# A fused attention and mixture-of-experts kernel: two start-up softmaxes taken head by head on ScalarE, four loads in another order, and three kinds of low parts moved at the pair hand-overs

## The chip, the core and the metric

One core of one Trainium2 chip runs the whole kernel. The metric is device time in microseconds (us), the median of repeated runs. The core has five queues of instructions, each of which runs in order: TensorE (PE, with its weight loads as PEld), VectorE (DVE), ScalarE (ACT), GpSimd (POOL) and SyncE (SP), which here issues every DMA. They wait for one another by semaphores.

## What is computed

```python
# attention over chunks of 64 tokens, 8 heads of 64, batch 8, 576 tokens each
scores = scale * np.matmul(q_c, k_c.transpose(0, 1, 2, 4, 3))      # scale = 1/8
scores = scores - np.max(scores, axis=-1, keepdims=True)
attn = np.exp(scores)
attn = attn / (np.sum(attn, axis=-1, keepdims=True) + 1e-09)
out = np.matmul(attn, v_c)
# x: 4608 tokens x 512; 4 experts, each 512 -> 1024 -> 512, weighted densely
p = domain_probs / (domain_probs.sum(-1, keepdims=True) + 1e-09)
for e in range(E):
    h = np.maximum(x @ w1[e], 0.0)
    out += p[:, e:e + 1] * (h @ w2[e])
```

All is fp32 at the outside.

## The kernel before

The 4608 tokens are nine blocks of 512. The first block is handled alone; the other eight form four pairs of blocks. The experts are cut into eight passes (`n_pass`: expert and half of the hidden width), so that the program is 40 passes: 8 for the first block, then 8 for each pair. Every matrix product is made of three fp32r products of a high part and a low part: `hi_part` is a cast on ScalarE, `lo_part` is a subtraction (source minus high part) on VectorE or GpSimd. From the first pair on, products of 1024 x 1024 are made with seven instead of eight block products (sums of blocks named s1 to s4 for weights, t1 to t4 for tokens), so blocks b11, b21, b22, t1 to t4 of the tokens need high and low parts each.

**The order is written by hand.** Inside `tc.manual_schedule()` each engine runs its instructions in the order of the code. Three places matter here.

*The start* (`load_all`, `startup`). Block 0 is four tiles of 128 tokens (t = 0 to 3). `load_all` issues the loads on SyncE. `startup` keeps TensorE busy with idle products (`keep_warm`, 128x512 in bf16 into a bank that nobody reads) until the first data is there. For tile 0 and tile 1: `start_scores` (32 products of 64x64 into one PSUM bank, 8 heads of 64 columns), `less_max` on VectorE (a maximum per head, L185, then its subtraction from all 512 columns, L187), `a_exp` on ScalarE (one exp of 128x512, L190), and `start_weights`, which is `a_norm` on VectorE: sum per head (L193), plus 1e-9 (L194), reciprocal (L196), product (L198). Then come transpose (L841, copied out of PSUM on ScalarE at L845), `start_values` (L854, attention times v), `start_x` (the high part of x, L278 on ScalarE) and `start_x_lo` (its low part, L281 on VectorE). `w1_split` makes the parts of a quarter of w1 (cast at L278, subtraction at L281). `start_hidden` makes the first products of w1 with x, for the tiles 0 and 1 together. Tiles 2 and 3 follow in the same way between these products.

*A pass* (`later_pass`). 28 steps, the list `WOVEN`, stand in TensorE's order: g and h are products of w1 (left) with token parts (right), a and b are products of w2 with the hidden parts of the pass ahead. Each is six matmuls of 128x512. Extra work is hung behind a step with `add(at, step, ...)`. After an a or b step `Outer.add` (L697) adds the PSUM bank to the accumulator on VectorE; the next product into the same bank waits for that.

*The hand-over from pair to pair.* In the last pass of a pair (`last_pass and more`, twice in the program: pair 1 to pair 2 after pass 23, and once more after pass 31; the first pair gets its parts elsewhere) the token parts of the next pair are made from `xraw` with the methods of `Tokens`: t2 lies in the two tiles `e` and `pt` (`sum2_apart`) and gets its parts in `split2` (L441) at step 20. The parts that are needed last are made in the list `late`, which is hung into the steps of the following pass: low part of t3 behind step 1, of t4 behind step 4, of b22 behind step 7. The first pass of the new pair reads t2 at step 4 (g6), t1 at step 6 (g5), t3 at step 9 (g7), t4 at step 11 (g4), b22 at step 12 (g3).

Of the kernel before, what the change touches and what calls it, by code (L numbers as in the profile page):

```python
# [15 lines left out]
P = 128  # L16
C = 64
# [4 lines left out]
NK = 4  # L22
HF = 512

WAITS = {"loads": 7, "softmax": 14, "copy": 2}
PAIR = 2
N_RAW = 6

# [2 lines left out]
def chunk_attention_moe(ctx: ExitStack, tc: tile.TileContext, qk, v, v0, dp, w1, w2, out):  # L31
# [241 lines left out]
    def w_loads(i, n, order=QUADS):  # L273
        for f, k in order:
            w_load(i, n, f, k)
# [7 lines left out]
    def split(eng, src, t):  # L283
        hi_part(src, t)
        lo_part(eng, src, t)
# [119 lines left out]
    class Tokens:  # L405
# [35 lines left out]
        def split2(self):  # L441
            i = self.KEYS["t2"]
            x_alloc(i)
            for k, t in enumerate(self.t2):
                split(nc.vector, t, [part[:, k] for part in xt[i]])

        def sum3(self, eng=None):
            self.less("t3", "b22", "b12", self.b12, eng)
# [365 lines left out]
    def start_load(t, step):  # L814
        for g in range(0, 2, step):
            b = slice(g, g + step)
            nc.sync.dma_start(
                out=qk0[t][:, b], in_=qk[t, b].rearrange("g c d x h s -> (c d) g x h s")
            )

    def start_v(t):
        nc.sync.dma_start(out=v0s[t // GT], in_=v0[:, t : t + GT])
# [76 lines left out]
    def load_all():  # L899
        start_load(0, 1)  # L900
        start_load(1, 2)
        start_v(0)
        start_load(2, 2)
        w_loads(0, 0)
        start_load(3, 2)
        start_v(2)
        nc.sync.dma_start(out=pr, in_=dp)
        w_load(1, 0, 0, 0)
        w_load(1, 0, 0, 1)

    def start_weights(t):
        es[t] = att.tile([P, 2 * HG, C], F32, name=("e", "pt")[t % 2])
# [2 lines left out]
    def startup(beside):  # L915
# [4 lines left out]
        keep_warm(WAITS["loads"], early)  # L920
        for t in range(2):
            start_scores(t)
            less_max(sc[t])
            a_exp(sc[t])
        start_weights(0)
        start_weights(1)
        keep_warm(WAITS["softmax"])
        start_transpose(0)
        for f, k in QUADS[:2]:
            w1_split(f, k, nc.gpsimd)  # L930
        keep_warm(WAITS["copy"])
        start_values(0)
        start_x(0)
        start_transpose(1)
        w1_split(1, 0, nc.gpsimd)
        start_x_lo(0)
        start_scores(2)
        less_max(sc[2])
        start_values(1)
        start_x(1)  # L940
        a_exp(sc[2])
        w1_split(1, 1, nc.gpsimd)
        start_x_lo(1)
# [283 lines left out]
    def later_pass(n, ahead, late, held):  # L1227
# [42 lines left out]
        if last_pass and more:  # L1270
# [11 lines left out]
            add(at, 26, lambda: x.hi("t4"))  # L1282
            late = [
                (0, lambda: x.hi("b22")), (0, lambda: first_load(pair + 2)), (1, lambda: x.lo("t3")),
                (4, lambda: x.lo("t4")), (7, lambda: x.lo("b22")),
            ]
        for i, name in enumerate(WOVEN):
            getattr(steps[name[0]], f"p{name[1]}")()
# [133 lines left out]
```

## Time and profile before

| what | before |
|---|---|
| median of three runs | 1523.82 us (1523.77 to 1523.97) |
| profiled execution | 1523.9 us, its span 1522.1 us (1.8 us lie around the span) |
| busy share of PE / DVE / ACT / POOL | 99% / 61% / 38% / 58% |
| chain that ended last | PE 94%, DVE 4%, DMA 1% |
| granted TensorE clock | 0.999 on the mean |

The profile is one execution on the chip. "Busy" is time in which an engine worked on an instruction; an idle time is put down to the instruction that ended it. The chain that ended last is followed back from the last instruction. Start times are counted from the start of the span.

### The profile page before, as it was taken

Reading aid. Unit: us, or ns where it says so; the run is one execution under the profiler, and the core shown is the slowest. Engines: PE = TensorE matmul, PEld = TensorE weight load, DVE = VectorE, ACT = ScalarE, POOL = GpSimd, SP = SyncE. Lnnn points to the kernel's source line nnn. Section 1 sums busy time; section 2 is a strip of 40 time slices with the busy share of each in tenths; the row PEclk is TensorE's granted clock in tenths of the full one; section 3 lists DMA queues with packets and bytes.
Section 4 is the critical chain, followed back from the end, with each engine's and each line's share of the span. In section 5 each row is a group of like instructions: output and inputs, shape, how many; then the busy total and the mean of one; then the engine's idle time right before and its main releaser. Section 6 shows DMA issues by size and latency. Waiting matters only on the chain.

```text
span 1522.1 us, 23390 instructions
## 1 busy us (share of the span) xinstructions
PE 1508.0 (99%) x8863; PEld 1239.0 (81%) x8863; DVE 922.0 (61%) x1290; ACT 573.1 (38%) x1000; POOL 875.7 (58%) x666
## 2 busy tenths in 40 slices
PE   8999999999999999999999999999999999999998
PEld 7888888888888888888888788888887788888887
DVE  5453554444444465776677956666668756666665
ACT  3343444344444434333333444333333443333332
POOL 2443578677666626555557654555557655555554
PEclk9999999999999999999999999999999999999999
DMA  6353349777677576766666667666666676666664
GB/s 196 125 158 123 111 163 312 267 254 243 227 238 237 195 262 214 230 208 220 216 195 197 194 231 236 209 227 213 207 192 199 191 231 201 198 202 200 201 193 140
DMA packets 167920, 314.17 MB, mean 206 GB/s; under 512 B 14192, under 2 KB 84096, under 8 KB 167808
## 3 DMA queue, kind: packets, MB, share of 16 engines
q1 hardware_dynamic: 167808, 312.68, 63.6%
q8 instruction: 70, 1.15, 0.3%
q14 instruction: 42, 0.34, 0.1%
HBM read 244.39 MB, written 68.23 MB: 205 GB/s over the span
## 4 chain that ended last, share of the span: by engine, by line
PE 94%; DVE 4%; DMA 1%; issue 0%; ACT 0%; POOL 0%; SPq 0%; DVEq 0%; ACTq 0%
PE A L468 46%; PE C L468 27%; PE B L468 16%; PE psa L169 1%; DVE xl L281 1%; PE psa L140 1%; PE psa L160 1%; DVE acc L697 1%; DVE wraw L641 1%; DMA wraw<-in_w 1%; PE psa L783 0%; DVE wraw L635 0%; DVE B L670 0%; DVE xraw L438 0%; PE A L854 0%
## 5 line engine op out<-in xcount | busy, mean ns | idle before, releaser
L650 POOL TENSOR_TENSOR hfl<-wraw,hfh 128x512 fp32r<-128x512 f32 x288 | 377.1, 1325 | 221.2 <-ACT hfh L647 218.9
L468 PE MATMUL A<-xh,wf 128*128 128x512 f32 (+1 forms) x1112 | 380.7, 389 | 0.3 <-DVE acc L763 0.3
L468 PE MATMUL A<-hfh,wf 128*128 128x512 f32 (+1 forms) x768 | 271.0, 394 | 2.7 <-DVE acc L697 2.7
L647 ACT CAST hfh<-wraw 128x512 fp32r<-128x512 f32 x288 | 176.5, 622 | 214.7 <-DVE wraw L641 64.0
L468 PEld LDWEIGHTS A<-xh,wf 128*128 128x128 f32 x1112 | 207.9, 188 | 43.2 <-issue 0.4
L530 ACT COPY s<-A 128x512 f32<-128x512 f32 x192 | 112.8, 587 | 329.9 <-PE A L468 329.2
L468 PE MATMUL A<-xl,wf 128*128 128x512 f32 (+1 forms) x556 | 214.8, 387 | 0.0
L468 PE MATMUL C<-xh,wf 128*128 128x512 f32 (+1 forms) x592 | 202.9, 390 | 0.0
L468 PEld LDWEIGHTS A<-hfh,wf 128*128 128x128 f32 x768 | 144.2, 188 | 34.2 <-DVE acc L697 4.6
L697 DVE TENSOR_TENSOR acc<-A,acc 128x512 f32<-128x512 f32 x174 | 119.3, 686 | 78.7 <-PE A L468 78.2
L468 PE MATMUL A<-hfl,wf 128*128 128x512 f32 x384 | 149.5, 389 | 0.0
L468 PE MATMUL C<-hfh,wf 128*128 128x512 f32 x384 | 134.4, 391 | 2.1 <-DVE acc L697 2.1
L281 POOL TENSOR_TENSOR hfl<-wraw,hfh 128x512 fp32r<-128x512 f32 x64 | 86.0, 1373 | 82.9 <-ACT hfh L278 80.9
L468 PEld LDWEIGHTS C<-xh,wf 128*128 128x128 f32 x592 | 110.5, 188 | 22.9
L468 PE MATMUL B<-xh,wf 128*128 128x512 f32 (+1 forms) x376 | 124.6, 385 | 0.7 <-ACT xh L278 0.7
L281 POOL TENSOR_TENSOR wf<-wraw,wf 128x512 fp32r<-128x512 f32 x70 | 91.3, 1327 | 52.7 <-ACT wf L278 52.4
L468 PEld LDWEIGHTS A<-xl,wf 128*128 128x128 f32 x556 | 104.3, 188 | 21.2
L468 PE MATMUL C<-xl,wf 128*128 128x512 f32 (+1 forms) x296 | 114.1, 387 | 0.0
L641 POOL TENSOR_TENSOR wf<-wraw,wf 128x512 f32<-128x512 f32 x23 | 29.7, 1293 | 143.9 <-DVE wf L635 143.9
L697 DVE TENSOR_TENSOR acc<-C,acc 128x512 f32<-128x512 f32 x90 | 62.0, 690 | 63.0 <-PE C L468 57.5
L650 POOL TENSOR_TENSOR hfl<-wf,hfh 128x512 fp32r<-128x512 f32 x48 | 70.9, 1478 | 37.7 <-ACT hfh L647 37.4
L468 PEld LDWEIGHTS C<-hfh,wf 128*128 128x128 f32 x384 | 72.1, 188 | 17.9 <-DVE acc L697 3.0
(194 smaller groups left out, 2733.2 us busy)
## 6 DMA issues: line engine op xcount, KB each, us to landing
wf<-w SPq DMA_DIRECT2D x336, 512.0 KB, 4.0
wraw<-in_w SPq DMA_DIRECT2D x128, 256.0 KB, 4.0
w<-wf SPq DMA_DIRECT2D x112, 256.0 KB, 4.3
qk_in<-in_qk SPq DMA_DIRECT2D x32, 512.0 KB, 5.6
v_in<-in_v SPq DMA_DIRECT2D x32, 256.0 KB, 4.3
w<-hfl SPq DMA_DIRECT2D x32, 256.0 KB, 2.4
w<-hfh SPq DMA_DIRECT2D x32, 256.0 KB, 2.9
w<-hfh SPq DMA_DIRECT2D x48, 128.0 KB, 2.6
```

The lines of the kernel that those rows point to most:

```text
L140: nc.tensor.matmul(s["sc"][half, c, j], lhsT=s["x"][rows, g, 0, h], rhs=s["x"][rows, g, 1, h], start=True, stop=True,)
L160: nc.tensor.transpose(ps[:, j], s["e"][:, j].rearrange("p c k -> p (c k)"), ident)
L169: nc.tensor.matmul(av[half, c, j], lhsT=s["v"][rows, 2 * j + odd], rhs=s["pt"][rows, j, half], start=True, stop=True,)
L281: eng.tensor_tensor(out=t[1], in0=src, in1=t[0].bitcast(F32), op=ALU.subtract)
L468: nc.tensor.matmul(out, lhsT=lhs(k, a), rhs=rhs(k, b), start=first and i == 0, stop=last and i == len(parts) - 1, skip_group_check=not (fi ...
L530: nc.scalar.copy(out=t, in_=self.a)
L641: (eng or nc.vector).tensor_tensor(out=self.values[place, k], in0=self.values[a, k], in1=self.values[b, k], op=op)
L647: nc.scalar.copy(out=self.part(name, 0)[:, k], in_=self.values[name, k])
L650: (eng or nc.gpsimd).tensor_tensor(out=self.part(name, 1)[:, k], in0=self.values[name, k], in1=self.part(name, 0)[:, k].bitcast(F32), op=A ...
L697: nc.vector.tensor_tensor(out=acc[key], in0=src, in1=acc[key], op=ALU.add)
```

## The change

**At the start.** The exps of tiles 0 and 1 go to a new `start_exp`: VectorE takes the maximum of each head and multiplies it by -1/8 (128x8), and ScalarE takes exp(x/8 + that) head by head, eight instructions of 128x64, each with an accumulated sum of the head (`accum_out`). `start_norm` adds 1e-9, takes the reciprocal and multiplies. Subtraction and sum over 128x512 on VectorE are gone for these two tiles. The idle products ahead of the first transpose are 10 instead of 14. The loads of w1's first two quarters stand ahead of that of tile 2. The parts of these two quarters are made behind the copies of both tiles, the second's low part on VectorE instead of GpSimd, and the scores of tile 2 stand behind the values of tile 1.

**At the hand-overs.** `split2` makes t2's two low parts on GpSimd; the low parts of t4 and b22 stand behind steps 6 and 8 instead of 4 and 7.

```diff
-WAITS = {"loads": 7, "softmax": 14, "copy": 2}
+WAITS = {"loads": 7, "softmax": 10, "copy": 2}
...
-                split(nc.vector, t, [part[:, k] for part in xt[i]])
+                split(nc.gpsimd, t, [part[:, k] for part in xt[i]])
...
+        w_load(0, 0, 0, 0)
+        w_load(0, 0, 0, 1)
         start_load(2, 2)
-        w_loads(0, 0)
+        w_load(0, 0, 1, 0)
+        w_load(0, 0, 1, 1)
...
+    def start_exp(t):
+        a, scale = sc[t], 1.0 / C**0.5
+        m = small.tile([P, 2 * HG], F32, name="m3")
+        nc.vector.tensor_reduce(out=m, in_=a, op=ALU.max, axis=AX)
+        nc.vector.tensor_scalar_mul(m, m, -scale)
+        zs[t] = small.tile([P, 2 * HG], F32, name="z3")
+        for h in range(2 * HG):
+            nc.scalar.activation(
+                out=a[:, h], in_=a[:, h], func=AF.Exp, scale=scale,
+                bias=m[:, h : h + 1], accum_out=zs[t][:, h : h + 1],
+            )
+
+    def start_norm(t):
+        es[t] = att.tile([P, 2 * HG, C], F32, name=("e", "pt")[t % 2])
+        z = zs[t]
+        nc.vector.tensor_scalar_add(z, z, 1e-9)
+        nc.vector.reciprocal(out=z, in_=z)
+        nc.vector.tensor_tensor(
+            out=es[t], in0=sc[t], in1=z.unsqueeze(2).broadcast_to(sc[t].shape), op=ALU.mult
+        )
...
             start_scores(t)
-            less_max(sc[t])
-            a_exp(sc[t])
-        start_weights(0)
-        start_weights(1)
+            start_exp(t)
+        start_norm(0)
+        start_norm(1)
         keep_warm(WAITS["softmax"])
         start_transpose(0)
-        for f, k in QUADS[:2]:
-            w1_split(f, k, nc.gpsimd)
         keep_warm(WAITS["copy"])
         start_values(0)
         start_x(0)
         start_transpose(1)
-        w1_split(1, 0, nc.gpsimd)
+        w1_split(0, 0, nc.gpsimd)
+        w1_split(0, 1, nc.vector)
         start_x_lo(0)
-        start_scores(2)
-        less_max(sc[2])
         start_values(1)
         start_x(1)
+        start_scores(2)
+        w1_split(1, 0, nc.gpsimd)
+        less_max(sc[2])
         a_exp(sc[2])
...
-                (4, lambda: x.lo("t4")), (7, lambda: x.lo("b22")),
+                (6, lambda: x.lo("t4")), (8, lambda: x.lo("b22")),
```

What stands in a row on the engines now, at the three places that the prediction speaks of:

ScalarE at the start, before (A are the scores of tiles 0 and 1, B and the first A banks behind them their transposes and values, C the scores of tile 2, `s` the copied transposes, `wf` the high parts of w1, `xh` those of x; in brackets the semaphores waited for):

```order
L190 ACTIVATE A_249<-A_249 128x512 [waits DVE_49,PE_49]
L190 ACTIVATE A_270<-A_270 128x512 [waits DVE_49,PE_49]
L845 COPY s_322<-B_317 128x512 [waits PE_49]
L278 CAST wf_324<-wraw 128x2x256 [waits DMAHW5_49]
L278 CAST wf_327<-wraw 128x2x256 [waits DMAHW6_49]
L278 CAST xh_238<-B_332 128x4x128 [waits PE_49]
L845 COPY s_355<-B_350 128x512 [waits PE_49]
L278 CAST wf_357<-wraw 128x2x256 [waits DMAHW7_49]
L278 CAST xh_238<-A_381 128x4x128 [waits PE_49]
L190 ACTIVATE C_361<-C_361 128x512 [waits DVE_49]
```

ScalarE at the start, after:

```order
L924 ACTIVATE A_249,z_269<-A_249,m_266 128x64 [waits DVE_49,PE_49]
L924 ACTIVATE A_249,z_269<-A_249,m_266 128x64 [waits Activation_49] x7
L924 ACTIVATE A_278,z_298<-A_278,m_295 128x64 [waits DVE_49,PE_49]
L924 ACTIVATE A_278,z_298<-A_278,m_295 128x64 [waits Activation_49] x7
L845 COPY s_330<-B_325 128x512 [waits PE_49]
L278 CAST xh_238<-B_334 128x4x128 [waits PE_49]
L845 COPY s_357<-B_352 128x512 [waits PE_49]
L278 CAST wf_359<-wraw 128x2x256 [waits DMAHW4_49]
L278 CAST wf_362<-wraw 128x2x256 [waits DMAHW5_49]
L278 CAST xh_238<-A_366 128x4x128 [waits PE_49]
```

Sixteen exps stand where two stood, and all but the first of a tile wait for ScalarE's own semaphore, that is for the exp ahead of them; the casts of w1 moved behind both copies.

GpSimd at a hand-over, before (`hfl` are low parts of the hidden values, L650):

```order
L650 TENSOR_TENSOR hfl_8273<-wraw,hfh_8271 128x512
L650 TENSOR_TENSOR hfl_8300<-wf_8176,hfh_8298 128x512
L650 TENSOR_TENSOR hfl_8318<-wraw,hfh_8316 128x512
L650 TENSOR_TENSOR hfl_8333<-wraw,hfh_8331 128x512
L650 TENSOR_TENSOR hfl_8273<-wraw,hfh_8271 128x512
L650 TENSOR_TENSOR hfl_8333<-wraw,hfh_8331 128x512
```

The same after:

```order
L650 TENSOR_TENSOR hfl_8281<-wraw,hfh_8279 128x512
L281 TENSOR_TENSOR xl_8284<-e,xh_8283 128x512
L281 TENSOR_TENSOR xl_8284<-pt,xh_8283 128x512
L650 TENSOR_TENSOR hfl_8308<-wf_8184,hfh_8306 128x512
L650 TENSOR_TENSOR hfl_8326<-wraw,hfh_8324 128x512
L650 TENSOR_TENSOR hfl_8341<-wraw,hfh_8339 128x512
L650 TENSOR_TENSOR hfl_8281<-wraw,hfh_8279 128x512
L650 TENSOR_TENSOR hfl_8341<-wraw,hfh_8339 128x512
```

The two low parts of t2 now stand ahead of the five low parts that close the pass; the last two of these with one name (8333 before, 8341 after) are read by step a2 of the next pass.

VectorE in the first pass after a hand-over, before (the first `xl` is t4's, the second b22's):

```order
L697 TENSOR_TENSOR acc_5735<-B_8403,acc_5735 128x512
L670 TENSOR_TENSOR B_8413<-B_8413,s_8398 128x512
L635 SCALAR_TENSOR_TENSOR wraw<-B_8413,ws 128x512
L281 TENSOR_TENSOR xl_8362<-xraw,xh_8361 128x1024
L697 TENSOR_TENSOR acc_5820<-C_8439,acc_5820 128x512
L697 TENSOR_TENSOR acc_5843<-A_8377,acc_5843 128x512
L281 TENSOR_TENSOR xl_8387<-xraw,xh_8386 128x1024
L697 TENSOR_TENSOR acc_5843<-C_8439,acc_5843 128x512
```

The same after:

```order
L697 TENSOR_TENSOR acc_5743<-B_8411,acc_5743 128x512
L670 TENSOR_TENSOR B_8421<-B_8421,s_8406 128x512
L635 SCALAR_TENSOR_TENSOR wraw<-B_8421,ws 128x512
L697 TENSOR_TENSOR acc_5828<-C_8446,acc_5828 128x512
L281 TENSOR_TENSOR xl_8370<-xraw,xh_8369 128x1024
L697 TENSOR_TENSOR acc_5851<-A_8385,acc_5851 128x512
L697 TENSOR_TENSOR acc_5851<-C_8446,acc_5851 128x512
L281 TENSOR_TENSOR xl_8395<-xraw,xh_8394 128x1024
```

Each of the two low parts moved behind one addition of a C bank.

## Rows read from the trace of the kernel before

**Rows 1.** The page, busy time, share and count by engine.

```profile
PE 1508.0 (99%) x8863; PEld 1239.0 (81%) x8863; DVE 922.0 (61%) x1290; ACT 573.1 (38%) x1000; POOL 875.7 (58%) x666
```

**Rows 2.** What TensorE waited for in the span: us in total, times, longest.

```profile
PE A L468 <- DVE acc L697: 2.7, 2, 1.3
PE C L468 <- DVE acc L697: 2.1, 2, 1.1
```

**Rows 3.** Timeline of ScalarE, start: start us, us, what, [idle before <-releaser].

```profile
11.37 0.58 ACT L845 COPY s<-B 128x512 f32<-128x512 f32 x1 [1.91 <-PE B L841]
13.03 0.62 ACT L278 CAST wf<-wraw 128x512 fp32r<-128x512 f32 x1 [1.07 <-DMA wraw<-in_w]
```

**Rows 4.** Timeline of VectorE, start.

```profile
5.59 0.69 DVE L185 TENSOR_REDUCE m<-A 128x8 f32<-128x512 f32 x1 [4.18 <-PE A L830]
...
9.41 0.17 DVE L194 TENSOR_SCALAR psa<-psa 128x8 f32<-128x8 f32 x1
...
15.63 0.68 DVE L185 TENSOR_REDUCE m<-C 128x8 f32<-128x512 f32 x1
...
19.13 0.69 DVE L198 TENSOR_TENSOR e<-C,z 128x512 f32<-128x512 f32 x1
20.66 0.69 DVE L185 TENSOR_REDUCE m<-C 128x8 f32<-128x512 f32 x1 [0.84 <-PE C L830]
```

**Rows 5.** Timeline of TensorE, start.

```profile
12.01 1.15 PE L854 MATMUL B<-s,qk_in 64*64 64x64 f32 x32 [0.24 <-ACT s L845]
...
13.09 0.66 PE L841 MATMUL B<-ident,pt 128*128 128x128 f32 x4
13.67 1.15 PE L830 MATMUL C<-xraw 64*64 64x64 f32 x32
...
23.86 1.15 PE L854 MATMUL A<-s,ws 64*64 64x64 f32 x32 [0.23 <-ACT s L845]
```

**Rows 6.** Groups of ScalarE by shape: busy us, mean ns of one | idle.

```profile
L190 ACT ACTIVATE A<-A 128x512 f32<-128x512 f32 x2 | 1.2, 582 | 6.1 <-DVE A L187 6.1
...
L103 ACT COPY s<-B 128x128 f32<-128x128 f32 x1 | 0.3, 266 | 2.9 <-PE B L102 2.9
...
L919 ACT ACTIVATE first<-s 128x1 f32<-128x1 bf16 x1 | 0.2, 203 | 0.0
```

**Rows 7.** Timeline of VectorE at the first hand-over.

```profile
850.21 1.18 DVE L281 TENSOR_TENSOR xl<-e,xh 128x512 fp32r<-128x512 f32 x1
...
851.91 0.68 DVE L697 TENSOR_TENSOR acc<-A,acc 128x512 f32<-128x512 f32 x1
...
855.04 1.27 DVE L281 TENSOR_TENSOR xl<-qk_in,xh 128x1024 fp32r<-128x1024 f32 x1
...
866.91 1.63 DVE L281 TENSOR_TENSOR xl<-xraw,xh 128x1024 fp32r<-128x1024 f32 x1
868.47 0.68 DVE L697 TENSOR_TENSOR acc<-C,acc 128x512 f32<-128x512 f32 x1
```

**Rows 8.** Timeline of GpSimd at the first hand-over.

```profile
828.81 2.54 POOL L650 TENSOR_TENSOR hfl<-wraw,hfh 128x512 fp32r<-128x512 f32 x2
...
841.07 3.52 POOL L650 TENSOR_TENSOR hfl<-wraw,hfh 128x512 fp32r<-128x512 f32 x2 [3.27 <-ACT hfh L647]
...
853.92 1.30 POOL L650 TENSOR_TENSOR hfl<-wraw,hfh 128x512 fp32r<-128x512 f32 x1 [3.08 <-ACT hfh L647]
855.39 4.59 POOL L650 TENSOR_TENSOR hfl<-wraw,hfh 128x512 fp32r<-128x512 f32 x3 [0.17 <-ACT hfh L647]
```

**Rows 9.** Timeline of TensorE at the first hand-over: two stops, and steps a2 and g2.

```profile
852.65 0.50 PE L468 MATMUL A<-hfh,wf 128*128 128x512 f32 x1 [1.33 <-DVE acc L697]
...
859.84 0.39 PE L468 MATMUL B<-hfh,wf 128*128 128x512 f32 x1
...
861.19 0.39 PE L468 MATMUL B<-xh,wf 128*128 128x512 f32 x1
...
869.21 0.50 PE L468 MATMUL C<-hfh,wf 128*128 128x512 f32 x1 [1.05 <-DVE acc L697]
```

More of the change, by code (lines that the diff above doesn't have):

```diff
@@ L909, in load_all @@
         w_load(1, 0, 0, 1)
+    zs = {}
+    def start_exp(t):
[17 more added lines that the diff above has]
+        )
     def start_weights(t):
```

## The prediction

> **What bounds the kernel now.** I read the page's busy times first: TensorE is busy for 1508.0 of the 1522.1 us of the span, VectorE for 922.0, ScalarE for 573.1, GpSimd for 875.7 [rows 1]. So nothing but TensorE's idle time can be won, 14.1 us in all. Second, what TensorE waited for: the two largest items are two kinds of stop before an addition of VectorE, 2.7 us in 2 times and 2.1 us in 2 times [rows 2], one of each kind at either hand-over between pairs. The rest of the idle time lies in the start and at the end. The change touches the start and the hand-overs, so I read both from the timelines. At the start TensorE is not lost to its own work but to a chain that goes round all engines (scores, maximum, exp, norm, transpose, copy, values), and it ends with the values of tile 2 at 23.86 us [rows 5]; behind that TensorE runs without a gap worth naming, so what this point moves, the end moves.
>
> **The start.** The old chain has for each tile a maximum, a subtraction and one exp of 0.58 us [rows 6]. The new one has a maximum (0.69) and a product of 128x8, which I take at the 0.17 of the like instruction [rows 4]; with hand-offs of some 0.05 the first exp begins at 5.59 + 0.69 + 0.17 + 0.07 = 6.52 us, where the old one began 0.6 us later. Then come sixteen exps on ScalarE, one behind the other, since each waits for the one ahead (the order, second list). Call the time from one to the next c. No row shows an exp with a bias from memory and a sum beside it. ScalarE's rows fall with the columns, 0.582 for 512 and 0.266 for 128 [rows 6]; the same slope gives 0.21 for 64, with a hand-off of 0.04 c = 0.25, the low end. If giving out the sum takes an instruction of its own, as long as the shortest on ScalarE, 0.203 [rows 6], and its hand-off, c = 0.49, the high end. I see no reason for either end and take the middle, 0.37.
>
> The Trainium skill has a rule that speaks against the change (ScalarE: Activation LUTs, section Rules for kernel authors): some 0.3 us for every ACTIVATE with a bias as a [128,1] pointer, plus 0.83 ns an element, which for 64 columns would be an estimated 0.35, and c an estimated 0.39. The rows of this kernel, whose bias is no pointer, lie lower (0.582 for 512 columns, where the rule would say 0.72), so no run here shows it yet; the sum would come out 0.3 us higher by it.
>
> ScalarE runs in order, so the first copy of a transpose stands behind both tiles' exps: S = 6.57 + 16c, which is 12.5 us at c = 0.37 against 11.37 [rows 3]. From S on: values of tile 0 begin 0.64 later (as 11.37 to 12.01) and take 1.15, transpose of tile 1 0.66 [rows 5], its copy until S + 3.1, values of tile 1 until S + 4.3, scores of tile 2, now behind them, until S + 5.4. VectorE meanwhile: ScalarE casts w1's first quarter at S + 2.95, GpSimd begins the low part at S + 3.6 and needs 1.27, half of 2.54 [rows 8]. VectorE's low part of the second quarter is due at S + 4.1, but the two engines take turns on such instructions (a GpSimd pair takes 3.52 instead of 2.54 beside VectorE's [rows 8]), so it runs to S + 5.5, the low part of x's first tile to S + 6.1, and the maximum of tile 2 starts there. Before, that maximum started at 15.63, the norm of tile 2 ended at 19.82, then VectorE waited 0.84 for the scores of tile 3, and from that maximum at 20.66 to the values at 23.86 it is 3.20 [rows 4, 5]. In the new order the scores of tile 3 are done earlier (S + 8.6) than the norm of tile 2 (S + 10.3), so the wait is gone: 4.19 + 3.20 = 7.39. The values of tile 2 begin at S + 13.5 = 20.07 + 16c, against 23.86: **a loss of 16c - 3.8**, which is 0.2 at the low end, 2.1 at 0.37, 4.0 at the high end. The chain won 0.6 on VectorE and lost it on ScalarE, and moving tile 2's scores behind tile 1's values lengthened it.
>
> What else the start changes costs nothing while this holds. w1's first half loaded earlier: before, ScalarE waited for it until 13.03 [rows 3] with both copies queued behind; now the cast is not due before S + 2.95 = 15.4, so the load is early in either order, and at c = 0.25 (13.5) still not late. Tile 2's load is 0.5 MB later; its scores ran at 13.67 without a wait [rows 5] and are due at S + 4.3 = 16.8. On SyncE the w2 loads that reuse w1's buffers are issued some 2 us later, and their casts are later as well. Four idle products fewer only shorten filling. The norms (0.17, then about 0.9) end before TensorE asks for them.
>
> **The hand-overs.** The first stop, 1.33 at 852.65 [rows 9], ended with the addition of 851.91, which stands 1.70 us behind the start of t2's low parts at 850.21 [rows 7]. Without them it ends 1.70 earlier and the stop is gone. But the two go to GpSimd at 1.27 each. GpSimd was idle for 3.08 us there, until 853.92, and then did four low parts, the last until 859.98 [rows 8]. That fits, but VectorE gets its turns in between. From 849.6 (853.92 - 3.08 - 1.27) GpSimd now has seven of 1.27, 8.9 us, and in it two of VectorE's 512-column sums at some 0.6 and t1's low part at some 1.2 (rows of 0.68 and 1.27 with their overlap [rows 7]): it ends at about 860.9, 0.9 later than before. Step a2 reads that last low part in the fifth of its six matmuls; they lie (861.19 - 859.84) / 6 = 0.23 apart, so at 859.84 + 4 x 0.23 = 860.75 [rows 9]. So TensorE wins 1.33 at the first stop and gives it back at a2: 0 is my value. The bounds are 1.4 won, if GpSimd gets through ahead of VectorE, and 0.2 lost.
>
> The second stop, 1.05 at 869.21, waits for the C addition of 868.47; t4's low part stands right ahead of it and held it from 866.91, 1.56 [rows 7, 9]. Moved behind, the addition may be 1.56 - 1.05 = 0.5 later for other reasons before TensorE stops again. GpSimd's later turns delay t3's low part by about 0.5, so the stop all but vanishes: 1.0 won. Who waits next: t4's low part now delays the addition that the next A product waits for, and b22's (up to 2.4 us with a turn of GpSimd's) ends close to step g3, which reads it. For that 0 to 0.8 may be lost. A hand-over thus wins 1.0, bounds 0.2 to 2.4 (both stops whole), and there are two: **2.0 won, 0.4 to 4.8**.
>
> **The sum.** The profiled execution took 1523.9 us; its median sister runs 0.1 less. 1523.9 + 2.1 - 2.0 - 0.1 = **1523.9 us**: no difference that can be told, since a measurement of this kernel tells about 0.2%, 3.05 us, from no change.
>
> **The rivals.** (1) *Cheap exps*: c is 0.25 to 0.30, ScalarE overlaps what the rows suggest it doesn't. For: the fall of the rows to 0.266 at 128 columns. Against: sixteen waits in a row. The start loses 0.6, the hand-overs win 2.0: 1522.4. (2) *The hand-overs clear wholly*: GpSimd takes t2's parts in its idle 3.08 us, no stop comes back, 4.8 won. For: the gap is longer than two parts. Against: the turns, and a2's nearness. With c = 0.37 1521.1, with cheap exps 1519.6. (3) *The accumulated sums are dear*, the case that ends slower: every exp is followed by a second instruction and c is 0.49 or more. Its place is ScalarE between 6.5 us and the first copy; it is slower than before as soon as 16c - 3.8 exceeds the hand-overs' 2.0, c > 0.36, and by more than 0.2% from c = 0.55. At 0.49 the time is 1525.8, at 0.57 1527.1; with hand-overs that win only 0.4, 0.49 gives 1527.4. (4) *The stops only move*: b22's or GpSimd's parts come late and the hand-overs win 0.4 in all; 1525.5.
>
> **How the numbers follow.** Forecast (c from 0.31 to 0.45, 1 us won at a hand-over) 0.42; (1) 0.18; (2) 0.12; (3) 0.18; (4) 0.10. Faster by over 0.2% (below 1520.8) takes nearly all of (2) when the exps are not dear, and little else: 0.11. Slower by over 0.2% (above 1526.9) takes most of (3) and a part of (4): 0.15. The same 0.74. The range goes from 1520.9 (two clear hand-overs, middling exps) to 1527.0 (exps near 0.56).
>
> **What would show it.** Right: exps of tile 0 and 1 that begin near 6.5 and follow each other by 0.31 to 0.45; the first copy of a transpose near 12.5; the maximum of tile 2 near 18.6 and the values of tile 2 near 26 us. At 850 to 853 no stop of TensorE, but one of about 1 us in step a2 that GpSimd's low part ends; the stop at the third addition below 0.3. Wrong: a c outside 0.31 to 0.45, a cast of w1 that waits for its DMA, no stop in a2, or one before t4's or b22's product.

## The result, and the profile after

The changed kernel takes 1526.28 us (median of 22 executions, 1524.18 to 1527.45) against 1523.86 (22 of the kernel before): ratio 1.0013, 95% interval 1.0007 to 1.0019. That lies inside the 0.2% that the prediction called "no difference that can be told", and inside its range; the forecast of 1523.9 is 2.4 us too low. The interval lies wholly above 1, so the change is a small loss and not nothing. The executions do not scatter round the median. Nine lie at 1524.18 to 1524.62 (mean granted clock 0.999), two at 1525.8 and eleven at 1526.8 to 1527.5 (all thirteen at 0.996 or 0.997), and the median falls into the gap. The profiled execution (1527.19 us, span 1525.5) is one of the upper ones.

What TensorE waited for (us in total, times, longest), which answers [rows 2]:

```profile
PE B L841 <- DVE e L934: 2.1, 1, 2.1
PE B L468 <- POOL hfl L650: 1.6, 2, 0.8
...
PE C L468 <- DVE B L670: 0.7, 2, 0.3
PE A L468 <- DVE acc L697: 0.5, 2, 0.2
```

The two old items, 2.7 and 2.1 before an addition, have shrunk to 0.5 and nothing. GpSimd's 1.6 is new at the hand-overs, with 0.7 behind it. Two large waits are new in the start: 2.1 us before the first transpose and 1.5 before the first values (the latter in TensorE's timeline below).

**Hand-overs.** TensorE and GpSimd at the first one, timelines (start us, us, what, idle before and what ended it), against [rows 8, 9]:

```profile
860.97 0.50 PE L468 MATMUL A<-hfh,wf 128*128 128x512 f32 x1 [0.23 <-DVE acc L697]
865.71 0.50 PE L468 MATMUL B<-hfl,wf 128*128 128x512 f32 x1 [0.82 <-POOL hfl L650]
879.04 0.50 PE L468 MATMUL C<-xh,wf 128*128 128x512 f32 x1 [0.33 <-DVE B L670]
```

```profile
854.44 1.75 POOL L281 TENSOR_TENSOR xl<-e,xh 128x512 fp32r<-128x512 f32 x1
856.14 1.83 POOL L281 TENSOR_TENSOR xl<-pt,xh 128x512 fp32r<-128x512 f32 x1
```

0.23 + 0.82 + 0.33 = 1.38 stand where 1.33 + 1.05 = 2.38 stood [rows 9]: 1.0 won at a hand-over, 2.0 at the two, the forecast to the tenth. GpSimd's two new parts take 1.75 and 1.83 instead of 1.27; into each falls an instruction of VectorE with two inputs from SBUF (L438 until 855.02, L641 from 856.14 to 856.81).

**Start.** ScalarE's timeline, then the groups of its new instructions (busy us, mean ns of one):

```profile
7.30 0.29 ACT L924 ACTIVATE A<-A,m 128x64 f32<-128x64 f32 x1 [5.07 <-DVE m L921]
7.51 0.19 ACT L924 ACTIVATION_READ_ACCUMULATOR A<-A,m 128x1 f32 x1
7.74 0.29 ACT L924 ACTIVATE A<-A,m 128x64 f32<-128x64 f32 x1
...
10.36 0.29 ACT L924 ACTIVATE A<-A,m 128x64 f32<-128x64 f32 x1
...
10.67 0.28 ACT L924 ACTIVATE A<-A,m 128x64 f32<-128x64 f32 x1
...
14.03 0.57 ACT L845 COPY s<-B 128x512 f32<-128x512 f32 x1
```

```profile
L924 ACT ACTIVATE A<-A,m 128x64 f32<-128x64 f32 x16 | 4.6, 287 | 5.5 <-DVE m L921 5.1
L924 ACT ACTIVATION_READ_ACCUMULATOR A<-A,m 128x1 f32 x16 | 3.1, 193 | 0.0
```

Each exp is followed by a second instruction that gives out its sum, as the high end of the prediction assumed. From one exp to the next it is 0.44 us, except at one place: the first exp of tile 1, which waits for no exp ahead of it, starts 10.67 - 10.36 = 0.31 behind the last of tile 0. The sixteen fill 14.03 - 7.30 = 6.73 us, so c = 0.42 on the mean. The first copy of a transpose starts at 14.03 (forecast 12.5, before 11.37 [rows 3]).

TensorE in the same stretch, against [rows 5]:

```profile
4.28 1.97 PE L830 MATMUL A<-xraw 64*64 64x64 f32 x32
...
12.08 0.63 PE L841 MATMUL B<-ident,e 128*128 128x128 f32 x4 [2.14 <-DVE e L934]
...
14.66 1.97 PE L854 MATMUL B<-s,qk_in 64*64 64x64 f32 x32 [1.52 <-ACT s L845]
16.56 1.11 PE L841 MATMUL B<-ident,pt 128*128 128x128 f32 x4
...
29.22 1.15 PE L854 MATMUL A<-s,ws 64*64 64x64 f32 x32 [0.23 <-ACT s L845]
```

The ten idle products end at 12.08 - 2.14 = 9.94, and TensorE then stands still until 12.08. Behind that the same kinds of product take nearly twice as long as before: values of 32 instructions 1.97 instead of 1.15, a transpose 1.11 instead of 0.66. The values of tile 2 start at 29.22 instead of 23.86. The reason is in the view by stretches (stretch, us, TensorE's busy time, granted clock, DMA share and GB/s):

```profile
12.00:14.00 2.00, 1.06 (x6) 0.87 1.08 397
14.00:16.00 2.00, 1.34 (x26) 0.50 1.06 381
16.00:18.00 2.00, 1.67 (x16) 0.50 0.47 155
...
20.00:22.00 2.00, 2.00 (x40) 0.50 0.31 99
22.00:24.00 2.00, 2.00 (x12) 0.57 0.72 203
24.00:26.00 2.00, 2.00 (x41) 1.00 0.90 326
```

The granted clock is 0.50 of full speed, the 1.2 of TensorE's two levels (1.2 and 2.4 GHz), from 14 to 22 us. In the kernel before every one of these stretches reads 1.00, as here:

```profile
12.00:14.00 2.00, 1.99 (x46) 1.00 0.94 283
```

The span's account closes: the start loses 29.22 - 23.86 = 5.36, the hand-overs win 2.0, and the span grew by 1525.5 - 1522.1 = 3.4.

### The profile page after: what moved, and what is told of

Read it like the earlier page. It is cut to its first block, busy times and chain, and to the rows that moved or that the text cites. A ratio compares the mean times of both kernels' runs of the same rounds, so it can differ in the third digit from the quotient of the medians.

```text
span 1525.5 us, 23412 instructions
## 1 busy us (share of the span) xinstructions
PE 1511.6 (99%) x8859; PEld 1241.7 (81%) x8859; DVE 920.8 (60%) x1285; ACT 578.6 (38%) x1030; POOL 881.8 (58%) x669
## 3 DMA queue, kind: packets, MB, share of 16 engines
q8 instruction: 70, 1.15, 0.3%
## 5 line engine op out<-in xcount | busy, mean ns | idle before, releaser
L650 POOL TENSOR_TENSOR hfl<-wraw,hfh 128x512 fp32r<-128x512 f32 x288 | 379.7, 1334 | 211.7 <-ACT hfh L647 209.4
L468 PE MATMUL A<-xh,wf 128*128 128x512 f32 (+1 forms) x1112 | 380.4, 388 | 0.3 <-DVE acc L763 0.3
L468 PE MATMUL A<-hfh,wf 128*128 128x512 f32 (+1 forms) x768 | 270.5, 394 | 0.5 <-DVE acc L697 0.5
L468 PEld LDWEIGHTS A<-xh,wf 128*128 128x128 f32 x1112 | 207.8, 188 | 43.4 <-issue 0.4
L468 PE MATMUL A<-xl,wf 128*128 128x512 f32 (+1 forms) x556 | 214.6, 387 | 0.0
L468 PE MATMUL C<-xh,wf 128*128 128x512 f32 (+1 forms) x592 | 203.0, 390 | 0.7 <-DVE B L670 0.7
L468 PEld LDWEIGHTS A<-hfh,wf 128*128 128x128 f32 x768 | 144.1, 188 | 31.7 <-DVE acc L697 1.9
L697 DVE TENSOR_TENSOR acc<-A,acc 128x512 f32<-128x512 f32 x174 | 119.2, 686 | 78.7 <-PE A L468 78.2
L468 PE MATMUL A<-hfl,wf 128*128 128x512 f32 x384 | 149.4, 389 | 0.0
L468 PE MATMUL C<-hfh,wf 128*128 128x512 f32 x384 | 134.0, 390 | 0.0
L468 PEld LDWEIGHTS C<-xh,wf 128*128 128x128 f32 x592 | 110.4, 188 | 24.5 <-DVE B L670 1.5
L468 PE MATMUL B<-xh,wf 128*128 128x512 f32 (+1 forms) x376 | 125.2, 387 | 0.0
L468 PEld LDWEIGHTS A<-xl,wf 128*128 128x128 f32 x556 | 104.2, 188 | 21.2
L468 PE MATMUL C<-xl,wf 128*128 128x512 f32 (+1 forms) x296 | 114.0, 387 | 0.0
L641 POOL TENSOR_TENSOR wf<-wraw,wf 128x512 f32<-128x512 f32 x23 | 29.7, 1292 | 144.6 <-DVE wf L635 144.6
L697 DVE TENSOR_TENSOR acc<-C,acc 128x512 f32<-128x512 f32 x90 | 62.1, 690 | 63.3 <-PE C L468 57.6
L650 POOL TENSOR_TENSOR hfl<-wf,hfh 128x512 fp32r<-128x512 f32 x48 | 70.6, 1471 | 37.4 <-ACT hfh L647 37.1
L468 PEld LDWEIGHTS C<-hfh,wf 128*128 128x128 f32 x384 | 72.1, 188 | 15.1
```

The source lines that it names most:

```text
L468: nc.tensor.matmul(out, lhsT=lhs(k, a), rhs=rhs(k, b), start=first and i == 0, stop=last and i == len(parts) - 1, skip_group_check=not (fi ...
L641: (eng or nc.vector).tensor_tensor(out=self.values[place, k], in0=self.values[a, k], in1=self.values[b, k], op=op)
L650: (eng or nc.gpsimd).tensor_tensor(out=self.part(name, 1)[:, k], in0=self.values[name, k], in1=self.part(name, 0)[:, k].bitcast(F32), op=A ...
L697: nc.vector.tensor_tensor(out=acc[key], in0=src, in1=acc[key], op=ALU.add)
```

## The experiments

Theory: the hand-overs win 2.0; the sixteen exps and the new order cost about what the sum said, at full clock; on top of it TensorE's standing still lets its clock fall in a part of the executions. The rivals stand in the expectations. All times are medians; the kernel before, on the same chip each time, took 1524.05, 1524.05 and 1523.93 for the runs 1 to 4, 5 to 8 and 9 to 12.

| run | kernel | us (median, range) |
|---|---|---|
| 1 | before + hand-overs | 1521.85 (1521.51 to 1522.63) |
| 2 | before + start | 1529.23 (1526.29 to 1529.58) |
| 3 | after, idle products 18 and 9 | 1524.84 (1524.13 to 1525.10) |
| 4 | after, sums on VectorE | 1524.11 (1523.39 to 1526.13) |
| 5 | after, old exps | 1523.34 (1523.06 to 1523.76) |
| 6 | before + t2 on GpSimd | 1523.35 (1522.42 to 1523.77) |
| 7 | before + later steps | 1522.54 (1521.14 to 1523.04) |
| 8 | before, idle products 5 | 1524.53 (1524.00 to 1524.85) |
| 9 | after, idle products 10 and 9 | 1524.35 (1524.08 to 1526.53) |
| 10 | after, idle products 18 and 2 | 1524.41 (1524.05 to 1525.13) |
| 11 | run 1 + w1's first half first | 1521.27 (1520.90 to 1521.53) |
| 12 | run 11 + t2 shared out | 1522.10 (1521.91 to 1522.51) |

**Runs 1 and 2: each half of the change alone.**

```diff
# run 1, on the kernel before
-                split(nc.vector, t, [part[:, k] for part in xt[i]])
+                split(nc.gpsimd, t, [part[:, k] for part in xt[i]])
-                (4, lambda: x.lo("t4")), (7, lambda: x.lo("b22")),
+                (6, lambda: x.lo("t4")), (8, lambda: x.lo("b22")),
# run 2: the rest of the change, without these two
```

> Only the hand-over part of the change (t2's low parts on GpSimd, t4's and b22's behind steps 6 and 8); the start is that of before. Theory (the parts add: the start loses, the hand-overs win 1.0 us each): 1521.9 us, 2.0 below before, with stops of about 0.2, 0.8 and 0.3 us per hand-over where before had 1.3 and 1.1. Rival (the hand-overs win nothing and the start loses only what the whole change lost): 1523.9 us.

> Only the start part of the change; the hand-overs are those of before. Theory: 2.0 us above the changed kernel, at two levels of about 1526.4 us (clock stays) and 1529.2 us (clock falls to its lower level from 14 to 23 us). Rival (the hand-overs win nothing): 1524.4 and 1527.2 us, the levels of the changed kernel.

Run 1: 1521.85, ratio 0.9985 (0.9976 to 0.9994), 2.2 faster; the stops are 0.24, 0.83 and 0.33 again. Run 2: 1529.23, ratio 1.0029 (1.0018 to 1.0040), six executions at 1529.1 to 1529.6 and two at 1526.3 and 1526.8, the latter at a mean clock of 1.000. The halves add up level by level (1526.3 - 2.2 and 1529.2 - 2.2 against 1524.4 and 1527.2), and the two levels belong to the start.

**Run 3: the changed kernel with more idle products.**

```diff
-WAITS = {"loads": 7, "softmax": 10, "copy": 2}
+WAITS = {"loads": 7, "softmax": 18, "copy": 9}
```

> The changed kernel with 18 instead of 10 idle products ahead of the first transpose and 9 instead of 2 behind it, so that TensorE is busy while ScalarE makes the exps. Theory (the serial exps cost some 2.5 us by themselves, the fall of the clock another 2.8 us in those runs that have it): granted clock 1.00 throughout, all runs near 1524.4 us. Rival A (the clock is the whole loss): near 1521.9 us. Rival B (the clock has nothing to do with TensorE's idle time): two levels as before, 1524.4 and 1527.2 us.

1524.84 and no upper level; the granted clock is 1.00 in every stretch from 4 to 28 us. ScalarE's copy and TensorE's values of tile 2, from their timelines:

```profile
13.51 0.58 ACT L845 COPY s<-B 128x512 f32<-128x512 f32 x1
```

```profile
26.53 1.15 PE L854 MATMUL A<-s,ws 64*64 64x64 f32 x32 [0.91 <-ACT s L845]
```

So at full clock the start loses 26.53 - 23.86 = 2.67, where the prediction had 2.1; 5.36 - 2.67 = 2.7 of the profiled execution's loss are not there when the clock stays up.

**Run 4: exps by heads, sums by VectorE.**

```diff
-                bias=m[:, h : h + 1], accum_out=zs[t][:, h : h + 1],
+                bias=m[:, h : h + 1],
+        nc.vector.tensor_reduce(out=z, in_=sc[t], op=ALU.add, axis=AX)
```

> The changed kernel without accumulated sums: the exps by heads keep the bias, the sums of the 8 heads are one reduction per tile on VectorE, as before. Theory (the read of the accumulator is a quarter of the price): from one exp to the next 0.33 instead of 0.435 us, the first copy of a transpose 1.7 us earlier, 1522.7 us where the clock stays. Rival (the sixteen waits set the price, not the read): the distance stays above 0.40 and the time at 1524.4 us or above.

Two levels again, six executions at 1523.4 to 1524.1 and five at 1525.4 to 1526.1. ScalarE's timeline:

```profile
7.30 4.99 ACT L924 ACTIVATE A<-A,m 128x64 f32<-128x64 f32 x16 [5.08 <-DVE m L921]
12.54 0.59 ACT L845 COPY s<-B 128x512 f32<-128x512 f32 x1 [0.25 <-PE B L841]
```

Without its sum an exp costs 4.99 / 16 = 0.31, so the sum costs 0.11 of the 0.42. The wait for the exp ahead costs about as much: within a tile two exps without sums stand 0.32 apart, at the border of the tiles, where there is none, 0.21 (9.55 to 9.76); with sums it was 0.44 and 0.31. The rival had named these waits, and no run leaves them out. The copy comes 1.49 earlier instead of 1.7, since the sums stand on VectorE ahead of the norms and the copy now waits for TensorE's transpose. The lower level falls by 0.8 only. In the profiled executions the rest shows at the end: from the last copy of the output out of PSUM to the end of the span it is 5.1 here and 4.4 in the changed kernel, and why the last stores land later here no run shows.

**Run 5: the changed kernel with the old exps.**

```diff
-            start_exp(t)
-        start_norm(0)
-        start_norm(1)
+            less_max(sc[t])
+            a_exp(sc[t])
+        start_weights(0)
+        start_weights(1)
```

> The changed kernel, with its load order, its order of steps and its hand-overs, but with the old softmax for tiles 0 and 1 (subtraction, one exp of 128x512 on ScalarE, sum on VectorE). My theory: the sixteen exps are the price, and the new order of steps costs about 1 us of its own; the first copy of a transpose is back near 11.4, the values of tile 2 start 13.5 behind it, near 24.9 against 23.86, and with hand-overs that win 2.0 the time is 1522.9, with no level above it, since TensorE's idle time ahead of the first transpose is near 1.2 us and not 2.1. Rival A: the order costs nothing, all of the loss is the exps': values of tile 2 near 23.9 and 1521.9. Rival B: the four idle products that are gone are the price: granted clock at 0.5 in some windows and 1524 to 1525.5 in a part of the executions.

1523.34, in one level; ScalarE and TensorE:

```profile
11.72 0.58 ACT L845 COPY s<-B 128x512 f32<-128x512 f32 x1 [1.91 <-PE B L841]
```

```profile
11.05 0.63 PE L841 MATMUL B<-ident,e 128*128 128x128 f32 x4 [1.13 <-DVE e L198]
...
24.77 1.15 PE L854 MATMUL A<-s,ws 64*64 64x64 f32 x32 [0.90 <-ACT s L845]
```

Loads and order alone cost 1523.34 - 1521.85 = 1.5 against run 1; rival A falls, and rival B, since the clock reads 1.00 throughout although the idle products are only 10 here too: TensorE stood still for 1.13 us ahead of the transpose, not for 2.14. By the medians the exps then add 1.1 (to the lower level, 1524.4) and the clock 2.8 (to the upper, 1527.2). The traces share it out otherwise. From the copy to the values of tile 2 run 1 takes 23.44 - 11.53 = 11.91 and run 5 13.05, so 1.1 is lost in the start; the last stores land late here too (5.0 from the last copy to the end of the span, 4.4 in run 1), which is another 0.6. The exps then cost 26.53 - 24.77 = 1.8 in the start (run 3 against run 5).

**Runs 6 and 7: the two parts at the hand-overs apart** (the first or the second pair of lines of run 1's diff).

> The kernel before with one change, t2's two low parts on GpSimd; the low parts of t4 and b22 stand where they stood. My theory: the stop before the first addition (1.33) goes, but 1.07 come back (0.24 at an addition and 0.83 in step a2, which GpSimd's last low part ends), and the stop at the third addition (1.05) stays or grows by up to 0.5, since GpSimd's later turns delay VectorE's low part of t3; so 0.3 won to 0.3 lost at each hand-over, 1523.5 to 1524.6. Rival: the low parts on GpSimd are what wins, the late steps only avert a follow-up: 1522.

> The kernel before with one change, the low parts of t4 and b22 behind steps 6 and 8. My theory: the stop of 1.33 before the first addition stays, that of 1.05 goes, and some 0.3 appear at step g3 behind b22's low part; 0.7 to 1.0 won at each hand-over, 1522.1 to 1522.7. Rival: the two parts of the change need one another, and without the other one this wins under 0.3 at each: 1523.5 to 1524.0.

TensorE's stops at the first hand-over with t2's low parts on GpSimd, and then with the later steps:

```profile
855.89 0.50 PE L468 MATMUL A<-hfh,wf 128*128 128x512 f32 x1 [0.21 <-DVE acc L697]
860.65 0.50 PE L468 MATMUL B<-hfl,wf 128*128 128x512 f32 x1 [0.82 <-POOL hfl L650]
869.23 0.50 PE L468 MATMUL C<-hfh,wf 128*128 128x512 f32 x1 [0.99 <-DVE acc L697]
```

```profile
852.40 0.50 PE L468 MATMUL A<-hfh,wf 128*128 128x512 f32 x1 [1.33 <-DVE acc L697]
873.70 0.50 PE L468 MATMUL C<-xh,wf 128*128 128x512 f32 x1 [0.36 <-DVE B L670]
```

Run 6 leaves 2.02 of 2.38 and takes 0.7 us off; its interval (0.9988 to 1.0005) does not tell it from before. Run 7 leaves 1.69 and takes 1.5 off (0.9981 to 0.9999). Each does by itself what it does together with the other: 0.36 + 0.69 = 1.05 against 1.0 for both.

**Run 8: the kernel before, TensorE left idle.** No work is changed; nine idle products are left out.

```diff
-WAITS = {"loads": 7, "softmax": 14, "copy": 2}
+WAITS = {"loads": 7, "softmax": 5, "copy": 2}
```

> The kernel before, with 5 idle products instead of 14 ahead of the first transpose: the work of the kernel is untouched, TensorE only stands idle for some 2.1 us longer there. My theory: idle time of that size ahead of the first transpose is what lets the granted clock fall to its lower level; windows of 0.5 behind 12 us, and 1526 to 1527 in a part of the executions (the rest at 1524). Rival: the idle time is harmless by itself and the clock falls for the exps' sake: 1524.0 in all, clock 1.00 in every window from 4 to 28 us.

1524.53: half right. The transpose and the clock, from the timeline of TensorE and the view by stretches:

```profile
11.17 0.63 PE L841 MATMUL B<-ident,e 128*128 128x128 f32 x4 [2.21 <-DVE e L198]
...
16.39 1.10 PE L854 MATMUL A<-s,qk_in 64*64 64x64 f32 x32
```

```profile
12.00:14.00 2.00, 1.89 (x30) 0.50 1.06 383
14.00:16.00 2.00, 2.00 (x34) 0.66 1.09 391
16.00:18.00 2.00, 1.50 (x52) 1.00 1.02 358
```

The clock does fall without any of the new exps, in nine of eleven executions by their mean clock (0.998 against 1.000), so the rival is out. But it is back within 4 us, and costs some 0.5 (1524.4 to 1524.9 against 1524.0 and 1524.05 for the two that kept it, and two are few), not 2.7. My theory had left out that the price hangs on what stands behind the fall. TensorE is busy for 1.89 and 2.00 of 2 us here, for 1.34 to 1.67 in the changed kernel, with stops of 1.52 and 0.68 for ScalarE. That is not the whole reason: in run 4 it is busy for 1.76 and 2.00, the clock is back as soon (0.80, 0.50 and 0.85 from 12 to 18 us), and yet the levels lie 1.9 apart. What the rows of run 8 show is a wait that it could give up. In the kernel before, TensorE waited ahead of the values of tile 1:

```profile
15.53 1.15 PE L854 MATMUL A<-s,qk_in 64*64 64x64 f32 x32 [0.71 <-ACT s L845]
```

At the lower clock this wait is gone (16.39 above), whereas run 4 keeps one of 0.67 there.

**Runs 9 and 10: which idle time, and does work behind it shorten the fall?** The changed kernel with 10 idle products ahead of the first transpose and 9 behind it; then with 18 and 2.

> The changed kernel with 10 idle products ahead of the first transpose, as it has, and 9 instead of 2 behind it. TensorE thus still stands idle for some 2.1 us ahead of the transpose, but hardly in the 1.5 us behind it. My theory after the run with 5 idle products: the idle time lets the granted clock fall, and how long it then stays at the lower level, which is the price, hangs on how much TensorE does behind it; so the clock falls, is back near 16 to 18 us instead of 24, and the executions lie at 1524.2 to 1525.3, with no level at 1527. Rival A: once fallen, the clock stays down until 24 us whatever stands behind: levels at 1524.4 and 1527.2 as in the changed kernel. Rival B: the idle time behind the transpose is what makes it fall: clock 1.00 throughout.

> The changed kernel with 18 idle products ahead of the first transpose instead of 10, and the 2 behind it as they were. TensorE has no idle time of over 0.5 us ahead of the transpose, but stands for 1.5 us behind it and 0.7 later. My theory: the 2.1 us ahead of the transpose are what lets the clock fall; without them it stays at 1.00, or falls for 2 us at most, and all executions lie at 1524.1 to 1525.1. Rival: any wait of over a microsecond is enough, with the thin work behind it: levels up to 1527 as in the changed kernel.

Run 9, stretches, and TensorE's timeline behind the first transpose:

```profile
12.00:14.00 2.00, 2.00 (x9) 0.64 1.08 389
14.00:16.00 2.00, 2.00 (x6) 0.50 1.05 395
16.00:18.00 2.00, 1.83 (x37) 1.00 0.87 290
```

```profile
12.37 3.79 PE L897 MATMUL C<-s 128*128 128x512 bf16 x9
16.09 1.15 PE L854 MATMUL B<-s,qk_in 64*64 64x64 f32 x32
```

The clock is back at 16 us, as I expected, and not at 24 (rival A) and not unbroken (rival B). The time is not what I expected: six executions lie at 1524.1 to 1524.4, five at 1526.3 to 1526.5. In the profiled execution, one of the five, the filling itself runs at the lower clock, nine products in 3.79 us, and the first values, whose operand is copied by 14.5, wait for them until 16.09. Whether the clock fell in the six others is not shown: the mean clock reads 0.999 in all eleven, so it does not tell a fall as short as this one. Run 10, stretch and the first values:

```profile
12.00:14.00 2.00, 0.62 (x4) 1.00 1.01 332
```

```profile
14.13 1.15 PE L854 MATMUL B<-s,qk_in 64*64 64x64 f32 x32 [1.51 <-ACT s L845]
```

With 18 products ahead, the clock stays at 1.00 although TensorE stands for 1.51 us behind the transpose; 1524.41, one level. The 2.1 us ahead of the first transpose are thus the place, and eight more idle products the cure. No run has the changed kernel with the 14 of before; four products of 0.23 (14 in 3.19 before) would leave an estimated 1.2 us of standing still, near the 1.13 at which run 5 kept its clock. What is left, 1524.41 against 1521.85, is the order and the exps.

**Runs 11 and 12: two attempts at a better version.** The load order by itself on top of run 1, then t2's low parts shared between VectorE and GpSimd.

```diff
# run 11, on run 1
+        w_load(0, 0, 0, 0)
+        w_load(0, 0, 0, 1)
         start_load(2, 2)
-        w_loads(0, 0)
+        w_load(0, 0, 1, 0)
+        w_load(0, 0, 1, 1)
# run 12, on run 11; the high parts stay in split2
+            add(at, 20, lambda: x.lo2(0, nc.vector))
+            add(at, 20, lambda: x.lo2(1, nc.gpsimd))
```

> The kernel before with the change at the hand-overs, and with w1's first two quarters loaded ahead of tile 2; nothing else of the start is changed. My theory: the casts of w1 no longer wait for their DMA (0.7 to 1.3 us before), so the second copy of a transpose comes 0.6 earlier, near 13.9, and tile 2's load, 0.5 MB later, is still in time; but TensorE has the scores of tile 2 in the place that this frees, so the values of tile 2 come only 0.1 to 0.5 earlier: 1521.4 to 1521.8, against 1521.85 without it. Rival: tile 2's load comes too late for its scores (13.8), and the time is 1522.3 or more.

> As the run before it (hand-overs as changed, w1's first two quarters loaded first), with t2's two low parts shared out: the first on VectorE, the second on GpSimd. My theory: the stop before the first addition is 0.6 to 0.8 (a single low part of 0.6 ahead of it, where two gave 1.33), that of 0.83 in step a2 goes, since GpSimd has one part of about 1.5 us less, and the 0.33 at step g3 stays: 1.0 to 1.1 at each hand-over instead of 1.4, 0.6 to 0.8 less in all: 1520.8 to 1521.2. Rival: the two engines take turns on the two parts, each is slower and neither stop goes: 1521.6 or more.

Run 11 is the fastest: 1521.27, ratio 0.9982 (0.9973 to 0.9991). ScalarE's casts of w1 start with the end of the copy, without a wait for a DMA (1.07 before [rows 3]):

```profile
12.37 1.14 ACT L278 CAST wf<-wraw 128x512 fp32r<-128x512 f32 x2
```

It is 0.6 below run 1, where 0.1 to 0.5 was expected; 0.1 of that is the difference of the two reference medians, and the intervals of the two ratios overlap. The profiled executions show less: from the copy to the values of tile 2 it is 23.46 - 11.88 = 11.58 against 11.91 in run 1, 0.3 won, but the copy comes 0.35 later and both spans are 1519.8. With the same loads and the same old exps run 5 took 13.05, so the new order by itself costs 1.5 in the start. Run 12 is 0.8 slower than run 11. TensorE's stops (its program has three lines more ahead, so L471 and L700 are L468 and L697):

```profile
851.26 0.50 PE L471 MATMUL A<-hfh,wf 128*128 128x512 f32 x1 [0.72 <-DVE acc L700]
856.07 0.50 PE L471 MATMUL A<-hfh,wf 128*128 128x512 f32 x1 [0.41 <-DVE acc L700]
873.05 0.50 PE L471 MATMUL C<-xh,wf 128*128 128x512 f32 x1 [0.37 <-DVE B L673]
```

The first stop is 0.72 and that for GpSimd in a2 is gone, both as expected; but with a2 on time the next A addition, queued behind a low part of t1, is late by 0.41, and the sum is 1.50 against 1.37 in run 11, 0.3 more at two hand-overs. The rest of the loss lies behind all work of the engines. The last copy of the output out of PSUM, in run 11 and then in run 12:

```profile
1515.37 0.42 DVE L1318 COPY s<-B 128x256 f32<-128x256 f32 x1 [0.53 <-PE B L1345]
```

```profile
1515.17 0.42 DVE L1323 COPY s<-B 128x256 f32<-128x256 f32 x1 [0.53 <-PE B L1350]
```

Run 12 is 0.2 ahead there (its start was 0.4 faster in this execution), and its span ends 0.5 later, at 1520.2 instead of 1519.8: the last two stores of 128 KB take 3.8 us to land instead of 2.9. Why they do, in runs 4, 5 and 12 alone, stays open; against sharing out t2's parts run 12 shows only the 0.3.

## Why the prediction was right, and where it was not

The verdict (no difference that can be told) was right because the two halves pull against each other, as the sum had them: -2.0 at the hand-overs, a loss at the start. In part that is luck. The start by itself lost 5.2 (run 2) where the sum had 2.1, about half of it by a term that the prediction did not have, the clock. The median of 1526.28 lies between the two levels, where no execution is, and nine of 22 executions lie above the range's upper end of 1527.0. Point by point:

- **Hand-overs, 2.0 won: right in the sum.** Runs 1, 6 and 7 and the profile show 1.0 each. Within it two terms were off and cancelled: t2's parts on GpSimd win 0.36 (value taken 0, since the give-back in a2 is 0.82 and 0.2 at the first stop, together less than 1.33), the later steps 0.69 instead of 1.0, since 0.33 to 0.36 come back at g3, behind b22's low part. The prediction had priced that as a possible 0 to 0.8 and put it at nothing in its value.
- **The time from exp to exp: the middle was low.** c is 0.42, where the prediction took 0.37 between 0.25 and 0.49. The mechanism that it kept for the high end, a second instruction for the sum (0.193, taken as 0.203), is there. The two overlap, so that a sum adds 0.11 to an exp's 0.31 (run 4). Of that 0.31 some 0.11 is the wait for the exp ahead, which the prediction had at a hand-off of 0.04. The 0.05 above the value taken are 0.8 us over sixteen exps. Together with a first exp 0.3 later than forecast (6.78 in run 3) and the 0.5 that the next point has too much, they make the 2.67 at full clock out of 2.1.
- **The Trainium skill's rule against the change** (ScalarE: Activation LUTs, section Rules for kernel authors): its estimated 0.35 for an exp of 64 columns is more than the 0.287 measured, and its estimated c of 0.39 less than the 0.42, as it has no word on the sum's own instruction.
- **From the copy to the values of tile 2, 13.5: right at full clock** (13.02 in run 3, 13.05 in run 5). Run 5 bears out the term that looked oddest, that the new order with its loads, without the exps, costs about 1 us in the start: 13.05 against 11.91 in run 1. Its median says 1.5, of which 0.6 lies in the last stores. One reading was off: before, only the second copy stood behind the casts of w1, not both, and the earlier load, put at nothing, wins 0.3 behind the first copy (run 11).
- **What failed: "Four idle products fewer only shorten filling."** The prediction counted them as filling that covers nothing. Here they also kept TensorE's clock up. With the longer chain of exps and fewer products, TensorE stands for 2.14 us, and in 13 of 22 executions the granted clock falls to its lower level. In the profiled one it stays there until 22 us, and from the copy to the values of tile 2 it takes 15.19 instead of 13.02 (run 3). Together with a first exp at 7.30 instead of 6.78 (scores of tile 0 in 1.97 instead of some 1.45 us), that is 15.19 - 13.02 + 7.30 - 6.78 = 2.7, the distance of the two levels. The 0.5 of the first exp is no part of the fall, which came later (run 5 had scores of 1.98 too and kept its clock), so the fall itself shows 2.2 here; whether every execution of the upper level has the late first exp as well is not shown. Run 8 shows the fall without the exps, runs 3 and 10 its absence with more filling.
- **The signs.** Exps spaced by 0.31 to 0.45, no stop at 850 to 853 (0.23 is left of it, at 860.97), a stop of about 1 us in a2 ended by GpSimd (0.82), none at the third addition: all seen. The first exp at 6.5 came at 7.30 in the profiled execution and at 6.78 in run 3. The copy at 12.5, the maximum of tile 2 at 18.6 and the values at 26 came out as 14.03, 22.08 and 29.22 in the profiled execution; at full clock as 13.51, 19.43 and 26.53. One of the signs for "wrong" showed as well, a stop behind b22's low part.

At the lower level the sum closes once the start is put in as measured at full clock: 1523.9 + 2.67 - 2.0 - 0.1 = 1524.5 against 1524.18 to 1524.62; the forecast of 1523.9 itself lies 0.3 below the fastest execution. What the upper level is worth to the median is that more than half of the executions lie there.

## What to carry to other kernels

Idle products can be more than filling: here a change that lengthened TensorE's wait had to lengthen what covers it, in the wait ahead of the transpose rather than behind it, where the filling ran at the lower clock and stood in the way of the work (runs 9 and 10). An accumulated sum on ScalarE was an instruction of its own, and each exp waited for the one ahead, so cutting one exp into eight with sums traded 1.39 us a tile on VectorE (less 0.17 for the new product) for 3.4 instead of 0.58 on ScalarE, an engine that runs in order with copies queued behind. And where a bundle comes out at nothing, run its parts: here the parts were -2.2 and +5, and the better version is the one with the hand-overs (1521.85), or with the load order as well (1521.27), which the intervals do not tell apart.

## What the hardware showed that I had not expected

- A little over 2 us in which TensorE stood still (2.14 and 2.21 in the profiled executions) were followed by the lower granted clock in most executions but not in all (by the mean clock 13 of 22 after; 9 of 11 in run 8); 1.5 us in run 10 and 1.1 in run 5 were not. What decides between executions of one kernel no run here settles.
- How soon the clock came back went with what TensorE did: within 4 us where it was busy for 1.76 to 2.00 of 2 us (runs 4, 8 and 9), some 10 us where it was stopped again by ScalarE (after). The price did not follow that time alone: the levels lie 1.9 apart in run 4 and some 0.5 in run 8, whose falls were about as long, and 2.7 after. The Trainium skill says that "activity releases the throttle" (TensorE: Matmul & The Clock Gate, section What's actually happening); the trace agrees in that, 2.00 of 2 us busy at 0.50 to 0.57 just ahead of 1.00.
- The granted clock reads 1.00 from 4 to 6 us in every run, yet tile 0's scores took 1.25 us in one execution and 1.97 in another. Where 1.00 stands so early, the products' own durations tell more.
- GpSimd's low part of 1.27 takes 1.75 to 1.83 when it meets an instruction of VectorE with two inputs from SBUF. The Trainium skill has the pair of ports that the two share as "an exclusive lock, not a bandwidth split" (SBUF — State Buffer, section SBUF: two separate sides). The rows fit: from the end of VectorE's L438 (855.02) and of its L641 (856.81) it is 1.17 and 1.16 to the ends of the two low parts, about one low part's own time.
- The end of the kernel differed by 0.7 us between programs that store the same way: 4.4 to 4.6 us from the last copy of the output to the end of the span in most, 5.0 to 5.1 in runs 4, 5 and 12. What is behind it no run here settles.
